# Where the transposes run: attention output by DMA, q and k by TensorE

## The chip, the cores and the metric

The kernel runs on one core of one Trainium2 chip. The metric is the device time of one execution in microseconds (us), and lower is better. Times of several runs of the same program are given with their median; the profile is of one of these executions and goes with that execution's own time.

## The reference

Inputs are q, k and v of shape (8 batches, 8 heads, 576 tokens, 64), and two weights, `moe_w_in` (512 x 2048) and `moe_w_out` (2048 x 512), all float32. Attention is causal within a window of 64 tokens; its output feeds a two-layer network:

```python
scores = (1/8) * q @ k.T                      # per batch and head
mask   = (rel >= 0) & (rel < 64)              # rel = query position - key position
attn   = softmax(where(mask, scores, -1e9))
x      = (attn @ v) -> (4608 tokens, 512)     # heads side by side
h      = x @ moe_w_in
g      = h * sigmoid(1.702 * h)
out    = g @ moe_w_out                        # float32
```

## The kernel before, in words

All matmul operands are bf16. The 4608 tokens are cut into 36 tiles m of 128 tokens, each of two query blocks of 64 tokens (nine blocks to a batch), and into nine chunks of four tiles, 512 tokens.

**Attention of one tile.** `scores(m)` (L243) makes 16 small matmuls, one per head and block: q of 64 tokens against k of 128 tokens, into the PSUM tile S. `exp(m)` (L253, ACT) writes E, `mask(m)` (L258, DVE) multiplies it with a 0/1 band into PT. `pv(m)` (L272) multiplies PT with v; a column of ones beside v gives the row sums. `norm(m)` takes the reciprocal of the sums (L283) and writes the tile xs, 128 tokens x 512, in bf16 (L285, DVE). `x_mm(m)` (L299) transposes xs by four TensorE transposes with the identity `ident` into the PSUM tile pxt, and `x_out(m)` (L307, DVE) copies that into xT, the chunk's transposed x (four blocks of 128 features x 512 tokens). Tacc of `pv` and pxt share one PSUM buffer (pool psT, one buffer).

**The network.** For a chunk ch and one of 16 hidden blocks f, `up_mm` (L318) makes four matmuls, 512 wide, from xT into hps (two buffers); `up_act` makes tanh (L329, ACT) and then gT (L331, DVE). `down_mm` (L338) makes matmuls from gT and w_out into ops (two buffers), 16 for each 128 tokens; `down_out` copies ops to o_sb (L348, ACT) and stores it from the SP queue (L349).

**Transposed q and k.** `scores` needs q and k with the head's 64 features on the partitions: qkt, two buffers, batch b in number b % 2. Two ways lead there.

- The first, for batches 0 and 1: `load_qk` (L74, on POOL's queue, with a cast to bf16) puts nine consecutive tokens in a row of a partition of `raw`. `spread` (L103, four copies on DVE) lays raw into `wide`, in which the other head's half is zero, and five units `qk_mm` (L205) transpose it on TensorE, with wide as weights against the 0/1 matrix `sel`: 16 matmuls in units 0 to 3, eight in unit 4. `qk_out` empties PSUM into qkt: for units 0 to 3 one copy on ACT (L220) and one on DVE (L222); for unit 4 one on ACT (L226), which writes every ninth token. From batch 1 on units use the PSUM tile S, of which there is one and which `scores` uses too. There is one `wide` for q and one for k, and `raw` has two buffers.
- The second, for batches 2 to 7: `load_rows` (L85, ten loads on POOL's queue, with a cast) puts tokens on the partitions, and `turn_rows` (L94, ten DMA transposes on the SP queue) writes qkt.

v comes by `load_v_f32` on the SP queue with `cast_v` on DVE and POOL for batches 0 and 1, and by `load_v` (L126, POOL's queue, with a cast) and `shift_v` (L133 and L134, DVE) later.

**Order.** Each engine runs its own instructions in the order in which the program states them; that order is written by hand. First come loads, the units of batch 0, and attention of tiles 0 to 3. Then a loop over 144 slots (chunk ch, block f): in each slot stand the works filed under `post` (ACT, DVE and DMA work), an output copy where f is a multiple of four, `up_mm` and `up_act` of (ch, f), the TensorE works filed under `pe`, and four `down_mm` of the chunk before. `at(slot, f, after)` files f under `pe` of its slot and `after` under `post` of the next; `later` files under `post`. `period` files scores of the next tile, pv of tile m, the mask, and x_mm two slots on. Tile m of 8 and more has slot 4(m - 4), so there is one attention tile to four slots; tiles 4 to 7 have slots 7, 9, 11 and 13. In the program's order `spread(1)` stands at slot 0, the units of batch 1 in slots 0 to 4. `load_v_f32(1)` is stated before the attention of tile 0.

Of the kernel before, what the change touches and what calls it, by code (L numbers as in the profile page):

```python
# [8 lines left out]
B = 8  # L9
H = 8  # L10
S = 576
D = 64
NTOK = B * S
DM = H * D
DFF = 2048
P = 128
NQB = 9
NM = NTOK // P
NCH = NTOK // 512
RR = 9  # L20
NT = S // RR
PAD = 64

fp32 = mybir.dt.float32
bf16 = mybir.dt.bfloat16
AF = mybir.ActivationFunctionType
ALU = mybir.AluOpType
# [3 lines left out]
def kernel(  # L31
# [9 lines left out]
    nc = tc.nc  # L41
    scale = 1.0 / 8.0

    keep = ctx.enter_context(tc.tile_pool(name="keep", bufs=1))
    ep_pool = ctx.enter_context(tc.tile_pool(name="ep", bufs=2))
    xs_pool = ctx.enter_context(tc.tile_pool(name="xs", bufs=2))
    rc_pool = ctx.enter_context(tc.tile_pool(name="rc", bufs=2))
    xt_pool = ctx.enter_context(tc.tile_pool(name="xt", bufs=3))
    th_pool = ctx.enter_context(tc.tile_pool(name="th", bufs=2))
# [3 lines left out]
    psT = ctx.enter_context(tc.tile_pool(name="psT", bufs=1, space=bass.MemoryType.PSUM))  # L53
# [10 lines left out]
    qkt = [keep.tile([P, 8, PAD + S], bf16, name=f"qkt{i}") for i in range(2)]  # L64
# [7 lines left out]
    def load_qk(b, hps):  # L72
        for w, src in enumerate((q, k)):
            nc.gpsimd.dma_start(  # L74
                out=raw[b % 2][w][:, hps, :],
                in_=src[b].rearrange("(g two) (p r) d -> (two p) g (r d)", two=2, r=RR)[:, hps, :],
            )

    rows = [[keep.tile([P, 5, DM], bf16, name=f"rows_{w}{i}") for w in "qk"] for i in range(2)]

    def load_rows(b):
        for w, src in enumerate((q, k)):
            for i in range(5):
                n = P if i < 4 else 64
                nc.gpsimd.dma_start(  # L85
                    out=rows[b % 2][w][0:n, i, :].rearrange("p (h d) -> p h d", d=D),
                    in_=src[b, :, P * i : P * i + n, :].rearrange("h p d -> p h d"),
                )

    def turn_rows(b):  # L90
        for i in range(5):
            for w in range(2):
                n = P if i < 4 else 64
                nc.sync.dma_start_transpose(  # L94
                    out=qkt[b % 2][:, w::2, PAD + P * i : PAD + P * i + n],
                    in_=rows[b % 2][w][0:n, i, :],
                )

    def spread(b, hps):
        for w in range(2):  # L100
            for par in range(2):
                rows = slice(par * 64, par * 64 + 64)
                nc.vector.tensor_copy(  # L103
                    out=wide[w][rows, hps, :, par, :],
                    in_=raw[b % 2][w][rows, hps, :].rearrange("p g (r d) -> p g r d", d=D),
                )
# [15 lines left out]
    def load_v(b):  # L122
        vn = v_nat[b % 2]
        for i in range(5):
            n = P if i < 4 else 64
            nc.gpsimd.dma_start(  # L126
                out=vn[0:n, i, :, 0:D],
                in_=v[b, :, P * i : P * i + n, :].rearrange("h p d -> p h d"),
            )
# [28 lines left out]
    for base in (0, -64):  # L158
        nc.gpsimd.affine_select(
            out=sel[:], in_=sel[:], compare_op=ALU.not_equal, fill=1.0,  # L160
            base=base, pattern=[[-1, 64]], channel_multiplier=1,
# [4 lines left out]
        out=band[:], in_=band[:], compare_op=ALU.is_ge, fill=0.0,  # L166
        base=64, pattern=[[1, 64]], channel_multiplier=-1,
    )
    nc.gpsimd.affine_select(
        out=band[:], in_=band[:], compare_op=ALU.is_ge, fill=0.0,  # L170
        base=-1, pattern=[[-1, 64]], channel_multiplier=1,
    )
    ident = keep.tile([P, P], bf16, name="ident")
    nc.gpsimd.memset(ident[:], 0.0)
    nc.gpsimd.affine_select(
        out=ident[:], in_=ident[:], compare_op=ALU.not_equal, fill=1.0,
        base=0, pattern=[[-1, P]], channel_multiplier=1,
    )
    for j in range(4):
        load_w_in(j)  # L180
# [47 lines left out]
    def blocks_of(m):  # L228
        return [(t, *divmod(2 * m + t, NQB)) for t in range(2)]

    def s_tile():
        return psS.tile([P, 2, 512], fp32, name="S", tag="S")

    S_of, PT_of, T_of, xs_of, E_of = {}, {}, {}, {}, {}
# [16 lines left out]
    def exp(m):  # L251
        E_of[m] = ep_pool.tile([P, 2, 512], bf16, name="E", tag="E")
        nc.scalar.activation(out=E_of[m][:], in_=S_of.pop(m)[:], func=AF.Exp, scale=scale)  # L253
# [11 lines left out]
    def pv(m):  # L265
        acc = T_of[m] = psT.tile([P, 2, 512], fp32, name="Tacc", tag="T")
        pt = PT_of.pop(m)[:].rearrange("p a f -> p (a f)")
        for h in range(H):
            for t, b, j in blocks_of(m):
                epos = (h % 2) * 512 + t * 256 + (h // 2) * 64  # L270
                win = (v_off if j % 2 == 0 else v_nat)[b % 2][:, j // 2, h, 0 : D + 1]
                nc.tensor.matmul(  # L272
                    acc[t * 64 : t * 64 + 64, h // 4, (h % 4) * 66 : (h % 4) * 66 + 65],
                    lhsT=pt[:, epos : epos + 64],
                    rhs=win,
                    start=True,
                    stop=True,
                )

    def norm(m):  # L280
        view = T_of.pop(m)[:, :, 0:264].rearrange("p b (h e) -> p b h e", e=66)
        rc = rc_pool.tile([P, 2, 4, 1], fp32, name="rc", tag="rc")
        nc.vector.reciprocal(out=rc[:], in_=view[:, :, :, D : D + 1])  # L283
        xs = xs_of[m] = xs_pool.tile([P, DM], bf16, name="xs", tag="xs")
        nc.vector.tensor_tensor(  # L285
            out=xs[:].rearrange("p (b h d) -> p b h d", b=2, h=4),
            in0=view[:, :, :, 0:D],
            in1=rc[:].to_broadcast([P, 2, 4, D]),
            op=ALU.mult,
        )  # L290

    xT = {}
    X_of = {}

    def x_mm(m):
        ps = X_of[m] = psT.tile([P, 4, P], bf16, name="pxt", tag="T")
        xs = xs_of.pop(m)
        for c in range(4):
            nc.tensor.transpose(  # L299
                out=ps[:, c, :], in_=xs[:, c * P : (c + 1) * P], identity=ident[:, :]  # L300
            )

    def x_out(m):
        ch = m // 4
        if m % 4 == 0:
            xT[ch] = xt_pool.tile([P, 4, 512], bf16, name="xT", tag="xT")
        nc.vector.tensor_copy(  # L307
            out=xT[ch][:, :, (m % 4) * P : (m % 4) * P + P], in_=X_of.pop(m)[:]
        )


# [40 lines left out]
    def pair(pool, shape_tag):  # L352
        return [pool.tile([P, 512], fp32, name="qk", tag=shape_tag)[:] for _ in range(2)]

    for u in range(5):
        if u % 2 == 0 and u < 4:
            spread(0, slice(u, u + 2))
        if u == 0:
            s = s_tile()
            p = [s[:, 0, :], s[:, 1, :]]  # L360
        elif u == 1:
            s = psT.tile([P, 2, 512], fp32, name="Tq", tag="T")
            p = [s[:, 0, :], s[:, 1, :]]
        elif u == 2:
            p = pair(psH, "H")
        elif u == 3:
            p = pair(psO, "O")
        else:
            p = [psH.tile([P, 512], fp32, name="qk", tag="H")[:]]
# [7 lines left out]
    for m in range(4):  # L377
        scores(m)
        exp(m)
        mask(m)  # L380
        if m > 0:
            x_mm(m - 1)
            x_out(m - 1)
        pv(m)
        norm(m)
    x_mm(3)
    x_out(3)

# [3 lines left out]
    def at(slot, f, after=()):  # L394
        pe.setdefault(slot, []).append(f)
        for g in after:
            post.setdefault(slot + 1, []).append(g)

    def later(slot, g):
        post.setdefault(slot, []).append(g)  # L400

    def qk_unit(slot, b, u):
        box = {}

        def mm():
            s = s_tile()
            box["p"] = [s[:, 0, :], s[:, 1, :]]
            qk_mm(b, u, box["p"])

        at(slot, mm, [lambda: qk_out(b, u, box["p"])])  # L410

    def period(slot, m, nxt):
        if nxt is not None:
            at(slot, lambda: scores(nxt), [lambda: exp(nxt)])
        at(slot, lambda: pv(m), [lambda: norm(m)])
        if nxt is not None:
            later(slot + 2, lambda: mask(nxt))
        at(slot + 2, lambda: x_mm(m), [lambda: x_out(m)])

    later(0, lambda: spread(1, slice(0, 4)))  # L420
    for u in range(5):
# [3 lines left out]
    def slot_of(m):  # L425
        return (7, 9, 11, 13)[m - 4] if m < 8 else 4 * (m - 4)

    for m in range(4, NM):
        period(slot_of(m), m, m + 1 if m + 1 < NM else None)

    for b in range(2, B):
        last_pv = slot_of((9 * (b - 1) - 1) // 2)
        later(last_pv + 1, lambda b=b: load_v(b))
        later(slot_of(9 * b // 2), lambda b=b: shift_v(b))
        turn_at = slot_of((9 * (b - 1) - 1) // 2 - 1) + 2
        later(turn_at, lambda b=b: turn_rows(b))
        later(5 if b < 4 else slot_of((9 * (b - 3) - 1) // 2 - 1) + 3, lambda b=b: load_rows(b))

    for ch in range(NCH):
        for f in range(16):  # L440
            s = 16 * ch + f
# [49 lines left out]
```

## Time and profile before

| | |
|---|---|
| time, three runs | 357.15 us median (355.5 to 358.89) |
| the profiled execution's own time | 358.89 us |
| its span, first to last instruction | 357.2 us |
| mean granted TensorE clock | 0.989 |
| PE busy | 304.4 us (85%), 2592 matmuls |
| DVE busy | 207.3 us (58%) |
| ACT busy | 151.7 us (42%) |
| POOL busy | 94.7 us (27%) |
| DMA moved | 36.47 MB in 134910 packets, 124128 of them under 512 B |

How to read it: PE is TensorE's matmuls and PEld its weight loads, DVE VectorE, ACT ScalarE, POOL GpSimd, and SP the queue that issues the stores and transposes. A row of a list in order of time gives start, duration, engine, source line, operation, output <- input, the count, and in brackets how long the engine was idle before and what ended that. A row of a group gives shapes and count, then the busy time in us and the mean of one in ns, then the idle time before. Matmuls are pipelined, so the distance between starts tells more of the time that they hold PE than the durations do.

### The profile page before, as it was taken

Reading aid. Unit: us, or ns where it says so; the run is one execution under the profiler, and the core shown is the slowest. Engines: PE = TensorE matmul, PEld = TensorE weight load, DVE = VectorE, ACT = ScalarE, POOL = GpSimd, SP = SyncE. Lnnn points to the kernel's source line nnn. Section 1 sums busy time; section 2 is a strip of 40 time slices with the busy share of each in tenths; the row PEclk is TensorE's granted clock in tenths of the full one; section 3 lists DMA queues with packets and bytes.
Section 4 is the critical chain, followed back from the end, with each engine's and each line's share of the span. In section 5 each row is a group of like instructions: output and inputs, shape, how many; then the busy total and the mean of one; then the engine's idle time right before and its main releaser. Section 6 shows DMA issues by size and latency. Waiting matters only on the chain.

```text
span 357.2 us, 6403 instructions
## 1 busy us (share of the span) xinstructions
PE 304.4 (85%) x2592; PEld 152.4 (43%) x2592; DVE 207.3 (58%) x339; ACT 151.7 (42%) x227; POOL 94.7 (27%) x118
## 2 busy tenths in 40 slices
PE   0034467767999999999999999999999999999995
PEld 0023333433444444444444444445444544444442
DVE  7876577675665675556655755566657565533400
ACT  1015213953445444555444444555454444444411
POOL 8061069954690026314921000010000000000000
PEclk9999998998999999999999999999999999999999
DMA  8999959999999299979994843771000000010021
GB/s 145 196 187 196 201 93 128 151 143 138 155 175 118 71 111 149 122 119 134 146 115 66 119 88 46 119 111 55 35 31 32 30 31 29 31 59 29 31 88 60
DMA packets 134910, 36.47 MB, mean 102 GB/s; under 512 B 124128, under 2 KB 130272, under 8 KB 134880
## 3 DMA queue, kind: packets, MB, share of 16 engines
q0 software_dynamic: 90752, 17.18, 61.1%
q1 hardware_dynamic: 44128, 18.88, 24.0%
q8 instruction: 20, 0.33, 0.4%
q14 instruction: 10, 0.08, 0.1%
HBM read 36.70 MB, written 9.44 MB: 129 GB/s over the span
## 4 chain that ended last, share of the span: by engine, by line
PE 74%; DVE 12%; issue 5%; ACT 4%; DMA 2%; POOL 2%; DVEq 0%; POOLq 0%; ACTq 0%
PE ops L338 33%; PE hps L318 30%; PE Tacc L272 4%; PE S L243 3%; DMA rows_k<-in_k_dram 2%; PE pxt L299 2%; DVE wide_k L103 2%; DVE v_off L133 2%; ACT qkt L226 1%; DVE v_off L192 1%; DVE v_nat L191 1%; POOL rows_q L85 1%; ACT E L253 1%; ACT th L329 1%; DVE PT L258 1%
## 5 line engine op out<-in xcount | busy, mean ns | idle before, releaser
L331 DVE SCALAR_TENSOR_TENSOR gT<-th,hps 128x512 bf16<-128x512 bf16 x144 | 99.0, 688 | 113.0 <-ACT th L329 112.6
L318 PE MATMUL hps<-xT,w_in_sb 128*128 128x512 bf16 x576 | 151.2, 387 | 2.4 <-DVE xT L307 2.4
L329 ACT ACTIVATE th<-hps 128x512 bf16<-128x512 f32 x144 | 86.3, 599 | 143.7 <-PE hps L318 137.9
L338 PE MATMUL ops<-w_out_sb,gT 128*128 128x512 bf16 x576 | 146.4, 381 | 0.0
L318 PEld LDWEIGHTS <-w_in_sb 128*128 128x128 bf16 x576 | 56.5, 99 | 69.9 <-issue 6.0
L338 PEld LDWEIGHTS <-gT 128*128 128x128 bf16 x576 | 53.0, 98 | 56.4 <-issue 0.8
L253 ACT ACTIVATE E<-S 128x1024 bf16<-128x1024 f32 x36 | 36.7, 1019 | 7.5 <-PE S L243 7.4
L85 POOL DMA_DIRECT2D rows_q<-in_q_dram x30 | 26.5, 892 | 50.2 <-DMA qkt<-rows_q 39.3
L126 POOL DMA_DIRECT2D v_nat<-in_v_dram x30 | 25.3, 869 | 52.1 <-PE Tacc L272 49.7
L348 ACT ACTIVATE o_sb<-ops 128x512 f32<-128x512 f32 x36 | 21.5, 597 | 20.0 <-PE ops L338 20.0
L85 POOL DMA_DIRECT2D rows_k<-in_k_dram x30 | 27.0, 924 | 4.2 <-DMA v_nat<-in_v_dram 2.5
L285 DVE TENSOR_TENSOR xs<-Tacc,rc 128x512 bf16<-128x512 f32 x36 | 24.9, 691 | 1.2
L205 PE MATMUL S<-sel,wide_q 128*128 128x64 bf16 x44 | 3.7, 242 | 22.7 <-DVE wide_q L103 20.2
L272 PE MATMUL Tacc<-v_off,PT 128*64 128x65 bf16 x320 | 17.4, 203 | 6.2 <-DVE xT L307 3.2
L258 DVE TENSOR_TENSOR PT<-E,mask_None 128x1024 bf16<-128x1024 bf16 x28 | 19.2, 685 | 2.0 <-ACT E L253 2.0
L272 PEld LDWEIGHTS <-PT 128*64 128x64 bf16 x576 | 13.7, 116 | 13.9 <-DVE PT L258 6.5
L243 PE MATMUL S<-qkt 64*128 64x64 bf16 x576 | 15.5, 196 | 4.2 <-ACT qkt L226 4.2
L272 PE MATMUL Tacc<-v_nat,PT 128*64 128x65 bf16 x256 | 15.1, 205 | 4.5 <-DVE xT L307 4.5
L243 PEld LDWEIGHTS <-qkt 64*128 64x128 bf16 x576 | 11.1, 98 | 17.1 <-issue 13.9
L205 PEld LDWEIGHTS <-wide_q 128*128 128x128 bf16 x72 | 5.2, 131 | 27.7 <-DVE wide_q L103 23.2
L299 PE MATMUL pxt<-ident,xs 128*128 128x128 bf16 x144 | 14.8, 229 | 2.5 <-DVE xs L285 2.5
L299 PEld LDWEIGHTS <-xs 128*128 128x128 bf16 x144 | 11.2, 102 | 10.7 <-DVE xs L285 3.3
(50 smaller groups left out, 113.4 us busy)
## 6 DMA issues: line engine op xcount, KB each, us to landing
out_dram<-o_sb SPq DMA_DIRECT2D x36, 256.0 KB, 2.1
rows_q<-in_q_dram POOLq DMA_DIRECT2D x24, 128.0 KB, 5.7
rows_k<-in_k_dram POOLq DMA_DIRECT2D x24, 128.0 KB, 6.2
v_nat<-in_v_dram POOLq DMA_DIRECT2D x24, 128.0 KB, 5.3
v_f<-in_v_dram SPq DMA_DIRECT2D x8, 256.0 KB, 12.5
w_in_sb<-in_moe_w_in_dram POOLq DMA_DIRECT2D x4, 512.0 KB, 14.0
w_out_sb<-in_moe_w_out_dram POOLq DMA_DIRECT2D x4, 512.0 KB, 14.8
raw_q<-in_q_dram POOLq DMA_DIRECT2D x2, 288.0 KB, 7.2
```

Source lines behind the costliest of these rows:

```text
L85: nc.gpsimd.dma_start(out=rows[b % 2][w][0:n, i, :].rearrange("p (h d) -> p h d", d=D), in_=src[b, :, P * i : P * i + n, :].rearrange("h p ...
L126: nc.gpsimd.dma_start(out=vn[0:n, i, :, 0:D], in_=v[b, :, P * i : P * i + n, :].rearrange("h p d -> p h d"),)
L243: nc.tensor.matmul(st[:, h % 2, t * 256 + hp * 64 : t * 256 + hp * 64 + 64], lhsT=src[rows, 2 * hp + 1, 64 * j : 64 * j + 128], rhs=src[ro ...
L253: nc.scalar.activation(out=E_of[m][:], in_=S_of.pop(m)[:], func=AF.Exp, scale=scale)
L258: nc.vector.tensor_tensor(out=pt[:].rearrange("p a f -> p (a f)"), in0=E_of.pop(m)[:].rearrange("p a f -> p (a f)"), in1=masks[z][:].rearr ...
L272: nc.tensor.matmul(acc[t * 64 : t * 64 + 64, h // 4, (h % 4) * 66 : (h % 4) * 66 + 65], lhsT=pt[:, epos : epos + 64], rhs=win, start=True, ...
L285: nc.vector.tensor_tensor(out=xs[:].rearrange("p (b h d) -> p b h d", b=2, h=4), in0=view[:, :, :, 0:D], in1=rc[:].to_broadcast([P, 2, 4, D]),
L299: nc.tensor.transpose(out=ps[:, c, :], in_=xs[:, c * P : (c + 1) * P], identity=ident[:, :])
L318: nc.tensor.matmul(ps[:, :], lhsT=w_in_sb[:, c, f * P : (f + 1) * P], rhs=xT[ch][:, c, :], start=(c == 0), stop=(c == 3),)
L329: nc.scalar.activation(out=th[:], in_=ps[:], func=AF.Tanh, scale=0.851)
L331: nc.vector.scalar_tensor_tensor(out=g[:], in0=th[:], scalar=1.0, in1=ps[:], op0=ALU.add, op1=ALU.mult)
L338: nc.tensor.matmul(O_of[ch, tsub][:, :], lhsT=gT[ch, f][:, tsub * P : (tsub + 1) * P], rhs=w_out_sb[:, f, :], start=(f == 0), stop=(f == 15),)
```

## The change

Batches 2 to 7 get q and k by the first way, as batches 0 and 1: `load_rows` and `turn_rows` go; `spread`, the five units and `qk_out` of each batch are filed in slots after `plan`. The units of batch 2 stand in slots 6, 8, 10, 12 and 14. For batches 3 to 7 units 0 to 3 stand two slots after an attention tile (slots 2, 6, 10 ... of four), unit 4 in the slot after unit 3, and that is the last slot before the first scores that need the batch. `spread(b)` is filed in the slot of unit 0, after the mask.

The attention output takes the DMA: `x_mm` and `x_out` go, with `ident`, and `x_turn(m)` issues one DMA transpose of xs into xT on the SP queue right after `norm(m)`. xs has four buffers in place of two.

```diff
-    xs_pool = ctx.enter_context(tc.tile_pool(name="xs", bufs=2))
+    xs_pool = ctx.enter_context(tc.tile_pool(name="xs", bufs=4))
...
-    def load_rows(b):
...
-    def turn_rows(b):
...
-    ident = keep.tile([P, P], bf16, name="ident")
...
-    def x_mm(m):
-        ps = X_of[m] = psT.tile([P, 4, P], bf16, name="pxt", tag="T")
-        xs = xs_of.pop(m)
-        for c in range(4):
-            nc.tensor.transpose(
-                out=ps[:, c, :], in_=xs[:, c * P : (c + 1) * P], identity=ident[:, :]
-            )
-
-    def x_out(m):
+    def x_turn(m):
         ch = m // 4
         if m % 4 == 0:
             xT[ch] = xt_pool.tile([P, 4, 512], bf16, name="xT", tag="xT")
-        nc.vector.tensor_copy(
-            out=xT[ch][:, :, (m % 4) * P : (m % 4) * P + P], in_=X_of.pop(m)[:]
+        nc.sync.dma_start_transpose(
+            out=xT[ch][:, :, (m % 4) * P : (m % 4) * P + P], in_=xs_of.pop(m)[:]
         )
...
         mask(m)
-        if m > 0:
-            x_mm(m - 1)
-            x_out(m - 1)
         pv(m)
         norm(m)
-    x_mm(3)
-    x_out(3)
+        x_turn(m)
...
-        at(slot, lambda: pv(m), [lambda: norm(m)])
+        at(slot, lambda: pv(m), [lambda: norm(m), lambda: x_turn(m)])
...
-        at(slot + 2, lambda: x_mm(m), [lambda: x_out(m)])
...
-    for b in range(2, B):
-        last_pv = slot_of((9 * (b - 1) - 1) // 2)
-        later(last_pv + 1, lambda b=b: load_v(b))
-        later(slot_of(9 * b // 2), lambda b=b: shift_v(b))
-        turn_at = slot_of((9 * (b - 1) - 1) // 2 - 1) + 2
-        later(turn_at, lambda b=b: turn_rows(b))
-        later(5 if b < 4 else slot_of((9 * (b - 3) - 1) // 2 - 1) + 3, lambda b=b: load_rows(b))
+    free = [s for s in range(14, 16 * NCH) if s % 4 == 2]
+    spare = [s for s in range(14, 16 * NCH) if s % 4 == 3]
+    first = {b: 4 * ((9 * b) // 2 - 5) for b in range(2, B)}
+    plan = {2: [(6, 0), (8, 1), (10, 2), (12, 3), (14, 4)]}
+    for b in range(3, B):
+        last = first[b]
+        slots = [s for s in free if s < last][-4:]
+        plan[b] = [(s, u) for u, s in enumerate(slots)]
+        plan[b].append(([s for s in spare if s < last][-1], 4))
+    for b, todo in plan.items():
+        later(todo[0][0], lambda b=b: spread(b, slice(0, 4)))
+        for s, u in todo:
+            qk_unit(s, b, u)
+        later(slot_of((9 * (b - 1) - 1) // 2) + 1, lambda b=b: load_v(b))
+        later(slot_of(9 * b // 2), lambda b=b: shift_v(b))
+    later(5, lambda: load_qk(2, slice(0, 4)))
+    for b in range(3, B):
+        later(plan[b - 2][-1][0] + 2 if b > 3 else 6, lambda b=b: load_qk(b, slice(0, 4)))
```

More of the change, by code (lines that the diff above doesn't have):

```diff
@@ L77, in load_qk @@
             )
-    rows = [[keep.tile([P, 5, DM], bf16, name=f"rows_{w}{i}") for w in "qk"] for i in range(2)]
-    def load_rows(b):
[L82 to L87, printed above, removed]
-                )
-    def turn_rows(b):
[L91 to L97, printed above, removed]
     def spread(b, hps):
@@ L171 @@
         base=-1, pattern=[[-1, 64]], channel_multiplier=1,
-    )
-    ident = keep.tile([P, P], bf16, name="ident")
[L174 to L177, printed above, removed]
     )
@@ L292 @@
     xT = {}
-    X_of = {}
-    def x_mm(m):
-        ps = X_of[m] = psT.tile([P, 4, P], bf16, name="pxt", tag="T")
-        xs = xs_of.pop(m)
-        for c in range(4):
-            nc.tensor.transpose(
-                out=ps[:, c, :], in_=xs[:, c * P : (c + 1) * P], identity=ident[:, :]
-            )
-    def x_out(m):
+    def x_turn(m):
         ch = m // 4
```

## The prediction

> **What bounds the kernel now.** I read the page's busy shares, then busy time by stage, then the order of time on PE, DVE and SP, then the groups for the pieces that the change multiplies. The stages (PE, PEld, DVE, ACT and POOL busy, clock, DMA share, GB/s; the DMA share can pass 1):
>
> ```profile
> 45.00:99.00 54.00, 39.91 (x412) 21.14 (x413) 36.85 (x58) 24.32 (x34) 37.80 (x41) 0.94 1.77 134
> 99.00:306.00 207.00, 206.37 (x1750) 100.86 (x1749) 124.22 (x217) 100.48 (x155) 42.69 (x51) 1.00 0.74 89
> ```
>
> From 99 us on PE is busy 206.4 of 207: each microsecond put on its queue, or each wait, lengthens the run. Before that PE idles 14 of 54 us. PE and DVE in order of time, one steady period:
>
> ```profile
> 131.96 1.03 PE L318 MATMUL hps<-xT,w_in_sb 128*128 128x512 bf16 x4
> 132.82 0.39 PE L299 MATMUL pxt<-ident,xs 128*128 128x128 bf16 x4
> 133.05 1.03 PE L338 MATMUL ops<-w_out_sb,gT 128*128 128x512 bf16 x4
> ...
> 132.53 0.68 DVE L258 TENSOR_TENSOR PT<-E,mask_None 128x1024 bf16<-128x1024 bf16 x1
> 133.65 0.69 DVE L331 SCALAR_TENSOR_TENSOR gT<-th,hps 128x512 bf16<-128x512 bf16 x1 [0.44 <-ACT th L329]
> ```
>
> The start-to-start times count, since matmuls overlap: four x transposes hold PE 133.05 - 132.82 = 0.23 us, four 512-wide matmuls 0.86. A slot is 4 up plus 4 down, 1.73 us. Between the mask and gT (0.44 us of idle DVE) the new copies will stand. The front, by SP, DVE and PE in order of time:
>
> ```profile
> 31.58 14.70 SPq L111 DMA_DIRECT2D v_f<-in_v_dram  x5
> 46.18 1.51 DVE L103 COPY wide_q<-raw_q 64x2304 bf16<-64x2304 bf16 x2
> 47.72 3.12 DVE L103 COPY wide_k<-raw_k 64x2304 bf16<-64x2304 bf16 x2
> ...
> 50.90 0.61 PE L205 MATMUL S<-sel,wide_k 128*128 128x64 bf16 x8 [2.29 <-DVE wide_k L103]
> ```
>
> SP issues batch 1's v until 46.28; and one spread of batch 1 (4.6 us on DVE) makes PE wait. That is the pattern the change repeats for six batches.
>
> **The Trainium skill.** "TensorE: Matmul & The Clock Gate", Part 2, step 1: matmuls stay in program order, only weight loads are pulled ahead. The trace agrees (the row at 50.90 stops the up matmuls behind it), so a PE wait for DVE can't be filled. Same page, "HAM oscillation": an idle stretch of about a window of 3.4 us halves the clock. Agrees in part: after 1.85 us without work at 83.6 to 85.46, and gaps before it, four down matmuls took 89.01 - 87.33 = 1.68 us, not 0.86; that spell lost 1.4 us. "VectorE: DVE Perf Modes", "The three transpose paths": TensorE is the shorter transpose, the DMA one 1309 ns. SP here holds 1.21 us for each 128x512 one, and landing takes longer still.
>
> **The change, part by part.** Sum made on the profiled execution: 358.89 us, span 357.2 and 1.7 around it.
>
> *Front* (up to the first up matmuls of chunk 1, now at 85.46). (a) Attention of m = 0 to 3: pv of m waits for the xT copy of m-1, a chain of 3.37 us per m (40.15 to 43.51). Without the copy 0.36 goes, three times, and the last xs ends at 44.1; but (b) shows that nothing can use it before 46.28: 0. (b) The four x transposes stand on SP behind batch 1's v, so none issues before 46.28. At the 1.3 us between transposes in the trace the fourth issues at 50.2. Landing took 2.3 us at the least, 2.5 to 3.4 (medians) late in the run, 7.7 beside the loads of 48 to 92 us; the new raw loads start at 50.2 too, so I take 4 (ends 2.3 and 7.7). Up of chunk 0 starts at 54.2, not 46.31: +7.9. (c) Slots 0 to 5 took 19.55 us. Spread of batch 1 now hides under that wait, and slot 0 falls from 5.0 to 2.56, and the rest keeps its order and its durations (batch 1's v casts, 3 us on DVE, and unit 4's 2.4 us copy among them): 16.8, so -2.7. (d) Slots 6 to 15 took 19.6. Spread of batch 2 stands between mask and gT at slot 6, and PE is stopped until 5.15 us into it, where two slots had taken 2.5. From there the one S tile passes from scores (exp 1.03) to a unit (ACT copy 0.59, then DVE 0.69, behind gT and mask): 4.2 us per pair of slots, as the 4.36 now. x of m = 7: norm ends 20.9 us after slot 6 starts, its DMA lands 3.5 later, so up of chunk 1 comes at 24.2: +4.6. The pxt and xT waits (7.8 us of pv waiting) go, but the S tile takes their place. Front: 7.9 - 2.7 + 4.6 = **+9.8**, ends +5 and +14 (mostly the landing, 2.3 to 7.7). If the wait in b were gone, spread 1 would lie open again: b and c go together.
>
> *Steady.* (e) 27 x 0.22 us of x transposes leave PE: -5.9. The xT copies (418 ns) leave DVE, which is not the bound: 0. (f) Batches 3 to 7 get 72 transposing matmuls each. At half clock 8 took 0.43 us (53.01 to 53.45), 54 ns each, which is the 64 columns; at full clock 27, I take 28: 5 x 72 x 28 ns = +10.1. Ends 27 and 54 (half clock kept, or the 128-column weight load binding): +9.7 and +19.4. (g) Spread. In the period shown it is queued after mask, so it starts 133.1; four copies of 0.76 us (1.51 for two) end at 136.2. The first unit stands on PE at 132.82 and its last eight matmuls wait for wide_k: it ends 136.45 instead of 133.27. Behind it stand the down matmuls and all later slots: 3.2 us per batch, +16. gT of that slot is late too, but its hps buffer is wanted two slots on: 0. In batches 3 and 5 POOL's next raw load is released by these copies, and its issue lies beside wide_k; beside POOL's cast one copy took 2.37 us, beside issues a half-size one 0.74 instead of 0.45: 0.5 twice, +1.0. Ends of g: 14 and 22. (h) Unit 4's ACT copy takes 2.4 us (row below) and holds both S and qkt, which the next slot's scores need. In the period shown tanh of unit 4's slot ends at 135.5, the copy at 137.9, and scores are due after up at 136.7: 1.2 us, five times, +6 (ends 4 and 8). The output copy and tanh queued behind it on ACT end at 139.1, gT at 139.8, before the up matmuls that want their buffer: 0 more. (i) Clock: a stop of 3.2 us is longer than the 1.85 that halved it; 1.4 us lost per spell, in three of five: +4 (ends 0 and 8). (j) x of the last m of a chunk: xs ends 3.4 us after its slot starts, the DMA lands 2.5 to 3.4 later, up wants it 7.7 after: hidden, 0; cover is 1 to 2 us, a landing of 5 would cost 0.7 at each of 7 chunks. On SP each transpose (1.21 us) stands one slot after an output store whose o_sb copy ends 0.6 us into the slot: no hold-up; a transpose waits for its xs with only the next store behind it. The new wait of xs for the transpose four tiles back is long over. On POOL raw loads of batch b+2 wait for spread of b, with v loads behind them that no one needs for 16 slots or more: 0. (k) SP loses 60 transposes, POOL the 60 row loads, 128 KB each in 256-byte pieces, and gets 12 of 576 KB: PE didn't wait for them after 99 us, so 0. (l) The copies of units 0 to 3, four of 0.69 us on DVE and four of 0.59 on ACT per batch, fall in the last slot of a period, where DVE has only gT and idles about 1 us of 1.73, ACT 0.9: they hide there, and S is free again before the next scores: 0; without that cover 0.7 us each.
>
> ```profile
> L226 ACT CAST qkt<-S 128x512 bf16<-128x512 f32 x1 | 2.4, 2403 | 0.0
> L103 DVE COPY wide_q<-raw_q 64x2304 bf16<-64x2304 bf16 x2 | 1.5, 750 | 0.0
> L103 DVE COPY wide_k<-raw_k 64x2304 bf16<-64x2304 bf16 x2 | 3.1, 1554 | 0.0
> ```
>
> Steady: -5.9 + 10.1 + 17 + 6 + 4 = **+31.2**. Together +41.0: 399.9 against 358.9. The median shown, 357.15, is 1.7 lower, so the forecast is 398.
>
> **Rivals.** *A, smaller stops:* transposes land in 2.3 us, so the front costs +5; DVE reaches the copies 1.2 us earlier (g = 10), h = 4, no clock loss: 5 - 5.9 + 10.1 + 10 + 4 = +23, about 380. For it: DVE is busy 124 of 207 us. Against: DVE works in order and the copies stand behind a mask. *B, everything dear:* beyond the forecast, front +4.2, f at 40 ns +4.3, the clock in all five spells +3, x late at each chunk +5, spread 1 dearer each time +5: +21.5, about 419. For it: landings of 7.7 and the 2.37 us copy; against: DMA share 0.74 in the steady part. *C, faster:* the front's 14 us of idle PE is made by the DMA share of 1.77 (row loads released late, shift of batch 2 waiting for v), and the change frees it. Price: -14, with -5.9 and +10.1, no other stop: 347. It decides if spread, unit 4 and the SP queue together stop PE less than 10 us. Against it: the waits in 65 to 85 us name DVE xT, not a DMA, and unit 0 already waited for spread. That x isn't turned by DMA is no case: all 36 transposes stand in the code.
>
> **How the numbers follow.** Forecast 0.62, A 0.16, B 0.18, C 0.04. Leaving out C and the outer half of A's and B's tails gives 377 to 415. Within 1% of 357 (about what a measurement can tell from no change) only a mixture with C's relief falls: 0.02; faster 0.03; slower 0.95.
>
> **What would show it.** Right: the first unit's matmuls waiting some 3 us for wide_k in six batches; scores waiting about 1.2 us for the 2.4 us copy; up of chunk 0 starting near 54 us, released by the transpose DMA; 72 matmuls per batch in 2.0 us; half-clock spells after the stops. Wrong: PE 99% busy from 105 us on, or up of each chunk waiting for xT. A front that ends before 90 us (up of chunk 1) speaks for A; matmuls of 50 ns for B.

## The result, and the profile after

The changed kernel takes 404.59 us (median of four runs, 401.52 to 405.18), beside 357.36 for the kernel before on the same chip: 1.1307 times as long, 95% interval 1.1228 to 1.1386. The forecast was 398, the range 377 to 415. The profiled execution took 404.34 us with a span of 402.5 and a mean granted clock of 0.975; the one before took 358.89 with 357.2 and 0.989. So 45.3 us of span have to be found between the two traces, where the prediction's sum said 41.0.

The border between its two parts, the first up matmuls of chunk 1, moved from 85.46 to 102.35 us. The front costs 16.9 us (forecast 9.8), the rest 28.4 (forecast 31.2): 300.15 us from there to the end, where 271.7 were.

Busy time by stage, after; the columns are those of the same view before (PE, PEld, DVE, ACT and POOL busy, clock, DMA share, GB/s):

```profile
45.00:116.00 71.00, 39.24 (x429) 20.37 (x430) 37.73 (x58) 26.70 (x37) 16.30 (x19) 0.88 0.79 103
116.00:351.00 235.00, 217.63 (x2033) 107.60 (x2032) 141.83 (x230) 122.67 (x183) 19.83 (x24) 0.99 0.41 68
```

PE was busy 206.4 of 207 us in the long stage; now it is 217.6 of 235. It works more and it also stops. Against the long stage before, the DMA share has fallen from 0.74 to 0.41 and POOL's busy time has halved; no gain in time shows from either.

The front in order of time, SP and PE, after:

```profile
31.93 15.46 SPq L91 DMA_DIRECT2D v_f<-in_v_dram  x5
47.43 5.23 SPq L272 DMA_TRANSPOSE xT<-xs  x4
...
58.87 1.87 PE L283 MATMUL hps<-xT,w_in_sb 128*128 128x512 bf16 x4 [15.37 <-DMA xT<-xs]
...
102.35 1.31 PE L283 MATMUL hps<-xT,w_in_sb 128*128 128x512 bf16 x4 [2.74 <-issue]
```

The four x transposes stand behind batch 1's v on SP, as step b said. The last is issued at 51.45, and PE, idle for 15.4 us, starts when it has landed, 7.3 us later. The three others took 2.4 to 2.8. Row 102.35 is the border, up of chunk 1. The landing of the four x tiles over this stretch, after:

```profile
DMA to landing us min/median/max: 2.4/2.6/7.3
```

One steady period in order of time (batch 6), PE above and DVE below, after:

```profile
238.25 1.03 PE L283 MATMUL hps<-xT,w_in_sb 128*128 128x512 bf16 x4
240.99 0.41 PE L179 MATMUL S<-sel,wide_q 128*128 128x64 bf16 x8 [1.72 <-DVE wide_q L83]
242.55 0.41 PE L179 MATMUL S<-sel,wide_k 128*128 128x64 bf16 x8 [1.15 <-DVE wide_k L83]
242.79 1.81 PE L303 MATMUL ops<-w_out_sb,gT 128*128 128x512 bf16 x4
...
238.82 0.68 DVE L232 TENSOR_TENSOR PT<-E,mask_None 128x1024 bf16<-128x1024 bf16 x1
239.42 1.52 DVE L83 COPY wide_q<-raw_q 64x2304 bf16<-64x2304 bf16 x2
240.97 1.52 DVE L83 COPY wide_k<-raw_k 64x2304 bf16<-64x2304 bf16 x2
```

This is the picture the forecast drew for step g: mask, four copies, and PE standing at each pair of them. Without the wait the unit would stand at 239.1 (238.25 and four matmuls) and end 0.46 later, at 239.6; it ends at 242.79, so 3.2 us are lost. The four matmuls from 242.79 on take 1.6 us and the next four, from 244.39, 1.7, not 0.86: the granted clock is 0.50 for a spell.

The waits of PE from 102.4 us on, after (total us, times, longest):

```profile
PE S L179 <- DVE wide_q L83: 8.6, 5, 1.7
PE S L179 <- DVE wide_k L83: 5.9, 5, 1.2
PE S L217 <- ACT qkt L200: 5.2, 5, 1.0
```

Five batches, three waits each, 19.7 us in all. The third line is step h. The copy that it waits for, after:

```profile
L200 ACT CAST qkt<-S 128x512 bf16<-128x512 f32 x7 | 16.9, 2411 | 0.0
```

### The profile page after: what moved, and what is told of

It reads as the page before. It is cut to its first block, busy times and chain, and to the rows that moved or that the text cites. A ratio compares the mean times of both kernels' runs of the same rounds, so it can differ in the third digit from the quotient of the medians.

```text
span 402.5 us, 6925 instructions
## 1 busy us (share of the span) xinstructions
PE 313.8 (78%) x2880; PEld 157.1 (39%) x2880; DVE 226.1 (56%) x351; ACT 176.4 (44%) x257; POOL 49.8 (12%) x68
## 4 chain that ended last, share of the span: by engine, by line
PE 66%; DVE 18%; ACT 9%; issue 4%; DMA 2%; SPq 1%; DVEq 0%; ACTq 0%
PE ops L303 29%; PE hps L283 27%; ACT qkt L200 4%; PE Tacc L246 4%; DVE wide_k L83 3%; PE S L179 3%; PE S L217 3%; DVE wide_q L83 3%; ACT th L294 3%; DVE PT L232 2%; DMA xT<-xs 2%; DVE gT L296 2%; ACT E L227 1%; DVE v_off L166 1%; DVE v_nat L165 1%
## 5 line engine op out<-in xcount | busy, mean ns | idle before, releaser
L283 PE MATMUL hps<-xT,w_in_sb 128*128 128x512 bf16 x576 | 153.7, 391 | 18.1 <-DMA xT<-xs 15.4
L303 PE MATMUL ops<-w_out_sb,gT 128*128 128x512 bf16 x576 | 148.1, 385 | 0.0
L283 PEld LDWEIGHTS <-w_in_sb 128*128 128x128 bf16 x576 | 56.3, 100 | 86.0 <-issue 24.2
L179 PE MATMUL S<-sel,wide_q 128*128 128x64 bf16 x260 | 15.2, 200 | 34.5 <-DVE wide_q L83 31.1
L194 ACT CAST qkt<-S 128x512 bf16<-128x512 f32 x29 | 17.0, 585 | 43.6 <-PE S L179 43.4
L179 PEld LDWEIGHTS <-wide_q 128*128 128x128 bf16 x288 | 15.2, 105 | 47.7 <-DVE wide_q L83 37.0
L313 ACT ACTIVATE o_sb<-ops 128x512 f32<-128x512 f32 x36 | 23.2, 643 | 19.1 <-PE ops L303 19.1
L217 PE MATMUL S<-qkt 64*128 64x64 bf16 x576 | 15.9, 199 | 12.9 <-ACT qkt L200 9.3
L196 DVE CAST qkt<-S 128x512 bf16<-128x512 f32 x29 | 20.0, 689 | 5.4 <-ACT qkt L194 5.4
L217 PEld LDWEIGHTS <-qkt 64*128 64x128 bf16 x576 | 12.0, 99 | 27.5 <-issue 21.6
L179 PE MATMUL S<-sel,wide_k 128*128 128x64 bf16 x260 | 15.3, 201 | 7.5 <-DVE wide_k L83 7.5
L179 PEld LDWEIGHTS <-wide_k 128*128 128x128 bf16 x288 | 13.5, 106 | 10.4 <-DVE wide_k L83 9.4
L200 ACT CAST qkt<-S 128x512 bf16<-128x512 f32 x7 | 16.9, 2411 | 0.0
## 6 DMA issues: line engine op xcount, KB each, us to landing
v_f<-in_v_dram SPq DMA_DIRECT2D x8, 256.0 KB, 12.6
```

The source lines that it names most:

```text
L179: nc.tensor.matmul(dst[:, col * 64 : col * 64 + 64], lhsT=wide[w][:, hp, r, :, :].rearrange("p two d -> p (two d)"), rhs=sel[:], start=Tru ...
L200: nc.scalar.copy(out=o, in_=i)
L217: nc.tensor.matmul(st[:, h % 2, t * 256 + hp * 64 : t * 256 + hp * 64 + 64], lhsT=src[rows, 2 * hp + 1, 64 * j : 64 * j + 128], rhs=src[ro ...
L283: nc.tensor.matmul(ps[:, :], lhsT=w_in_sb[:, c, f * P : (f + 1) * P], rhs=xT[ch][:, c, :], start=(c == 0), stop=(c == 3),)
L303: nc.tensor.matmul(O_of[ch, tsub][:, :], lhsT=gT[ch, f][:, tsub * P : (tsub + 1) * P], rhs=w_out_sb[:, f, :], start=(f == 0), stop=(f == 15),)
```

## The experiments

The first six kernels are the changed one with one edit each; two put edits together; the last two start from the kernel before. Ratios are to the kernel before, with 95% intervals. That kernel, run again beside each, had medians of 357.4 to 357.7, so the times can also be set beside the changed kernel's 404.59. Each trace is of a single execution.

### The wide copies earlier

```diff
-        later(todo[0][0], lambda b=b: spread(b, slice(0, 4)))
+        if b == 2:
+            later(todo[0][0], lambda b=b: spread(b, slice(0, 4)))
+        else:
+            for i in range(4):
+                before = 1 if i > 1 else 3 - b % 2
+                later(todo[0][0] - before, lambda b=b, i=i: spread_one(b, i))
```

> The changed kernel, but for batches 3 to 7 the four spread copies are filed one to three slots before the first unit, two and two, instead of in its slot; batch 2 is left. Forecast's theory (the stop before the first unit is the price, 3.2 us five times, and it brings two half-clock spells of 1.7 us): 404.6 - 16 - 3.4 + 1 to 2 for delayed gT = 386 to 388 us, PE's waits for wide in the steady part under 2 us, full clock there. Rival (DVE has no room, the copies only push gT and the masks, and PE waits for those instead): gain under 8 us, 397 or more, with PE waiting for gT or PT.

Measured: 385.52 us, ratio 1.0768 (1.0687 to 1.0848), 19.1 below the changed kernel. A unit of the same phase, PE in order of time, with the copies earlier:

```profile
223.97 0.40 PE L187 MATMUL S<-sel,wide_q 128*128 128x64 bf16 x8
224.20 0.40 PE L187 MATMUL S<-sel,wide_k 128*128 128x64 bf16 x8
224.43 1.03 PE L311 MATMUL ops<-w_out_sb,gT 128*128 128x512 bf16 x4
```

The 16 matmuls take 0.46 us, 29 ns each, and nothing waits. In the steady part the waits for wide, 14.5 us in the changed kernel, are all gone, and so is the half clock after them. All the copies are still done, and so are all the matmuls: what cost the time was the place of the copies, not their work. How much of the 19.1 us belongs to it is less sharp. The profiled execution, at 381.15 us the fastest of the four, is 23.2 below the changed kernel's; 6.2 of these lie in the front, which this edit leaves alone (up of chunk 1 at 96.16, not 102.35; "The turns before the loads" shows why), and 17.0 behind it. That is about the 16.1 of stops and 3.4 of half clock, less 1.5 for an x tile late at one chunk and 1.2 more of pv waiting for `v_off`.

### Batch 1's v by POOL's queue

```diff
-    load_v_f32(1)
...
+    load_v(1)
...
-    later(2, lambda: cast_v(1))
+    later(2, lambda: shift_v(1))
```

> The changed kernel, but v of batch 1 is loaded with a cast on POOL's queue and shifted, as v of batches 2 to 7, so that SP is free for the x transposes of tiles 0 to 3. Theory 1 (the transposes stand behind batch 1's v on SP, and that makes the first 12.6 us): they issue right after each norm, 35 to 44.5 us, land 2.5 to 3 us later, up of chunk 0 starts at 47 to 48 instead of 58.9, and the run takes 393 to 395 us. Theory 2 (the landing of 7.3 us beside the loads is the larger half, SP's queue only the smaller): the issue moves to 44.5, the landing stays 6 to 8 us since the weights' loads still run, up of chunk 0 at 51 to 53, 397 to 399 us. A rival for which neither counts, the front being held by DVE: 402 or more.

Measured: 400.12 us, ratio 1.1209 (1.1148 to 1.1271), 4.5 below. SP and PE in order of time, with v by POOL:

```profile
37.24 10.30 SPq L272 DMA_TRANSPOSE xT<-xs  x4
...
56.32 0.59 PE L283 MATMUL hps<-xT,w_in_sb 128*128 128x512 bf16 x1 [10.98 <-DMA xT<-xs]
```

SP is free, and the first transpose is issued ten microseconds earlier. The up projection still comes only 2.5 us earlier, because now all four land late (the trace has 7.9 to 11.1 us from issue to landing, 9.9 for the last): POOL's loads are under way all the while. Both theories expected more, in time and for chunk 0; theory 2 came nearer. At chunk 0, freeing SP's queue gains little, since the landing grows by most of what the queue gave back. The 2.5 us there, and the 4.2 by which up of chunk 1 comes earlier (98.13), are within the scatter of the front between executions, shown under "The turns before the loads".

### q and k alone

The q and k half of the change, with x transposed on TensorE as before (xs with two buffers, `ident`, `x_mm` and `x_out` put back).

> One half of the change alone: q and k of batches 2 to 7 by raw loads, spread and units as in the changed kernel, but x by four matmuls and a PSUM copy as before. Theory (nearly all of the loss is in the q and k half): the front gets back the 12.6 us before chunk 0 but shows spread of batch 1 again (+2.4) and pv waits for the xT copies beside the S tile (+2 to 4), so up of chunk 1 comes at 95 to 97; the steady part gets 27 x 0.22 = 5.9 us more on PE: 402 to 406 us, the same as the changed kernel. Rival (x's DMA is the main loss): 375 us or less.

Measured: 403.99 us, ratio 1.1306 (1.1233 to 1.1379): the change without its x half is as slow as the change. In its trace the span is 399.8 and up of chunk 1 starts at 93.28:

```profile
93.28 1.08 PE L299 MATMUL hps<-xT,w_in_sb 128*128 128x512 bf16 x4 [3.16 <-DVE xT L288]
```

So in the profiled executions the x half costs 9.1 us in the front (102.35 against 93.28) and saves 6.4 after it (306.5 against 300.15), where step e had 5.9. The 9.1 is of a slow front: other traces with the changed front have up of chunk 1 at 96.2 to 101.4. The medians, 0.6 apart, say that the two sides about cancel.

### The fifth unit's copy on two engines

```diff
-            nc.scalar.copy(out=o, in_=i)
+            if b < 3:
+                nc.scalar.copy(out=o, in_=i)
+            else:
+                nc.scalar.copy(out=o[:, 0:4], in_=i[:, 0:4])
+                nc.vector.tensor_copy(out=o[:, 4:8], in_=i[:, 4:8])
```

> The changed kernel, but unit 4's copy into qkt is halved for batches 3 to 7: four of the eight blocks on ACT, four on DVE. Theory (scores wait about 1.04 us five times for the 2.4 us ACT copy): ACT takes 1.2 us, DVE's half lies beside it if a strided 2-byte write costs it about the same, the waits go, 404.6 - 4 to 5 = 400 to 401 us. Rival (DVE's half comes later than ACT's whole did, since it stands behind gT, or its strided write is slow): scores wait for DVE instead, 404 or more.

Measured: 404.69 us, ratio 1.1319 (1.1230 to 1.1407); nothing gained, a miss. ACT, DVE and PE in order of time, with the copy split:

```profile
138.53 1.29 ACT L203 CAST qkt<-S 128x256 bf16<-128x256 f32 x1
139.85 1.28 DVE L204 CAST qkt<-S 128x256 bf16<-128x256 f32 x1 [0.51 <-ACT qkt L203]
141.19 0.41 PE L221 MATMUL S<-qkt 64*128 64x64 bf16 x16 [1.23 <-DVE qkt L204]
```

Each half takes half the time, but DVE, idle before, starts 0.03 us after ACT has ended: the sum is what it was. The Trainium skill's "PSUM — Partial Sum Buffer", in its section on PSUM bank collisions, says that two engines may not touch one bank on the same partitions at once, and that software puts a wait between them, for two readers too. The trace has such a wait, but does not show the bank to be its reason. DVE's copies of two other units in order of time, in the changed kernel:

```profile
28.40 0.69 DVE L196 CAST qkt<-qk 128x512 bf16<-128x512 f32 x1 [0.16 <-PE qk L179]
...
62.25 0.69 DVE L196 CAST qkt<-S 128x512 bf16<-128x512 f32 x1 [0.15 <-ACT qkt L194]
```

In the second (unit 0 of batch 1) ACT and DVE read different halves of S, 512 columns each, and DVE still starts 0.03 us after ACT has ended. In the first (unit 3 of batch 0) each half is a PSUM tile of its own, and DVE starts while ACT's copy runs on to 28.56, though both write the same qkt. So in these traces the wait goes with the shared PSUM tile. The fifth unit with two tiles was not run.

Why a copy of 512 columns takes 2.41 us here, and 0.585 in the other units, is not a matter of the engine: both halves are as slow on theirs. It writes every ninth token, 18 bytes apart, and the Trainium skill's "Advanced Engine Details and Errata", SBUF Cachelines, has a penalty where each access falls in another line of 16 bytes. The two durations would fit that; no run here changes the step.

### The fifth unit first

```diff
-        plan[b] = [(s, u) for u, s in enumerate(slots)]
-        plan[b].append(([s for s in spare if s < last][-1], 4))
+        slots.append([s for s in spare if s < last][-1])
+        plan[b] = list(zip(slots, (4, 0, 1, 2, 3)))
```

> The changed kernel, with the fifth unit of turns of batches 3 to 7 (the one whose ScalarE copy takes 2.4 us) done first of the five, two slots ahead, and the four others in the slots after it. The spread copies are filed with the first unit, as before. Theory 1, the 1.0 us stop of TensorE behind that copy is one of order only, since in the new place the next scores' tile is free in time or the copy lies beside more TensorE work: the five stops, 5.2 in the trace, go, and the time is 399-400. Theory 2, whichever unit has the copy, the scores of the next tile wait for it: 404-405, with the stop at another place.

Measured: 400.07 us, ratio 1.1177 (1.1126 to 1.1228), 4.5 below, near the 5.2 of the trace. In its trace the waits of scores for the 2.4 us copy are gone from the steady part, and the waits for wide stand (8.6 and 6.9 us, where they were 8.6 and 5.9). Step h was a matter of order. The profiled execution, at 401.82 us the slowest of the four, shows less of the gain: four of its five stops for wide are followed by half clock, not two, and the part after the border is only 1.6 shorter.

### The turns before the loads

POOL reads one column of each of the four x tiles, and so waits for them, before it issues batch 2's loads.

```diff
+    def hold():
+        for t in range(4):
+            nc.gpsimd.tensor_copy(out=held[:, t : t + 1], in_=xT[0][:, 0, P * t : P * t + 1])
+
+    held = keep.tile([P, 4], bf16, name="held")
+    later(5, hold)
     later(5, lambda: load_qk(2, slice(0, 4)))
```

> The changed kernel, with POOL made to wait for the four x tiles of chunk 0 before it issues batch 2's loads of q and k. In the changed kernel the fourth of those tiles landed 7.3 us after its issue, in the moment in which these loads begin, where 2.4 to 2.6 us are usual. Theory 1, the tile waits behind the loads' traffic: it lands in about 2.5, the up projection of chunk 0 starts near 54 in place of 58.9, and the time falls by 2 to 5, to 400-402. Theory 2, the landing has nothing to do with these loads: the up projection starts at 58 to 59 and the time stays at 404, or rises, since the loads come later and slot 6 waits longer for them.

Measured: 400.82 us, ratio 1.1181 (1.1107 to 1.1255), 3.8 below. PE busy, clock, DMA share and GB/s while the last tile is on its way, first in the changed kernel:

```profile
53.00:55.00 2.00, 0.00 (x0) 1.00 0.91 138
55.00:57.00 2.00, 0.00 (x0) 1.00 1.20 196
```

and with the turns before the loads:

```profile
53.00:55.00 2.00, 1.54 (x5) 1.00 0.03 8
```

In the first, POOL's raw loads begin at 51.14, just before the transpose, and the DMA engines fill up. In the second they are held until 53.64. Its landings, and the matmul that waited:

```profile
DMA to landing us min/median/max: 2.4/2.6/2.9
...
53.23 0.58 PE L283 MATMUL hps<-xT,w_in_sb 128*128 128x512 bf16 x1 [10.06 <-DMA xT<-xs]
```

All four land in under 3 us, and up of chunk 0 starts at 53.23 instead of 58.87; 0.8 of these 5.6 us come from SP, which was free earlier in this execution, and 4.8 from the landing. Only the loads' time of issue differs by the edit (and four tiny copies on POOL), so the loads are the cause of the late landing.

Other traces bear this out and show the scatter. The last of the four tiles took 2.4 to 2.5 us in all three traces with the hold (this one and the two below). Without it, in the four traces whose front is that of the changed kernel, the landing goes with the order of two issues: where POOL's first raw load was issued 0.2 to 0.3 us ahead of the last transpose, it took 7.3 (changed kernel) and 7.1 (fifth unit first); where the load was issued 0.2 to 0.3 us behind it, 4.2 (wide copies earlier) and 4.8 (copy on two engines). Up of chunk 0 started at 58.87, 57.92, 53.66 and 56.20. So a part of the front's cost is luck of the execution. The Trainium skill's "DMA: Bandwidth & Descriptors", Issuing engines are not separate DMA queues, says that DMAs of all issuing engines run on the same 16 DMA engines and interleave: a transpose on SP's queue is no way around POOL's loads.

### The amendments together

The early wide copies, the fifth unit first, the hold, and batch 2's wide copies one slot earlier.

```diff
+        if b == 2:
+            later(todo[0][0] - 1, lambda b=b: spread(b, slice(0, 4)))
...
+        plan[b] = list(zip(slots, (4, 0, 1, 2, 3)))
...
+    later(5, hold)
```

> The changed kernel with three amendments together: the wide copies of batches 3 to 7 filed one to three slots ahead of the first unit, two and two (batch 2's one slot ahead), the fifth unit first, and the loads of batch 2 held until the four x tiles of chunk 0 have landed. If the stops are separate terms they add up: 404.6 - 19 (wide copies) - 5 (fifth unit) - 3 (landing) - 3 (slot 6), 374 to 378. If one hides behind another: 380 to 386. If the change had no cost besides these, it would come to 357; what remains over that is the five units a batch themselves and the front.

Measured: 379.65 us, ratio 1.0597 (1.0546 to 1.0649), above the range in which the gains just add, and just below the other one. The weight load ahead of the first up matmul of chunk 1 in order of time, and the landing of that chunk's last two x tiles, in this kernel:

```profile
97.70 0.14 PEld L291 LDWEIGHTS <-w_in_sb 128*128 128x128 bf16 x2 [9.08 <-issue]
...
DMA to landing us min/median/max: 8.3/9.0/9.6
```

PE stops for 8.6 us there, where the changed kernel stops 2.7: chunk 1's last tile, issued at 88.1, met loads that POOL had issued from 79.4 to 90.6. So the amendments moved the loads from one turn on to another. A second hold, for chunk 1's tiles, ahead of the loads of q and k of batch 4 and of v of batch 3:

```diff
+    later(15, lambda: hold(1))
```

> The kernel with the three amendments together took 379.7, 2 to 6 above the sum of the single gains: its trace shows TensorE stopped for 8.6 us ahead of the up projection of chunk 1, with the last x tile of that chunk issued at 88.1 and landed 9.6 later, while POOL's loads (q and k of batch 4, v of batch 3) were under way. Here POOL waits, ahead of those loads, for the four x tiles of chunk 1, as it does for those of chunk 0 ahead of batch 2's. Theory 1, an x tile lands late because loads are under way: it lands in 2.5 to 3, 6 of the 8.6 go, and some of the half clock after the stop; 370 to 374. Theory 2, the late landing has another cause, or the loads only meet another tile: 378 to 381.

Measured: 374.37 us, ratio 1.0491 (1.0419 to 1.0563), 5.3 less, 0.4 above what theory 1 gave. The weight load again, and the landing of the last two x tiles, with the second hold:

```profile
93.36 0.14 PEld L291 LDWEIGHTS <-w_in_sb 128*128 128x128 bf16 x2 [5.01 <-DMA xT<-xs]
...
DMA to landing us min/median/max: 5.5/7.4/9.3
```

The last tile lands in 5.5 us instead of 9.6, where 2.5 to 3 were expected, and PE's stop is shorter by as much, 4.1 us, not by 6. Loads issued before 77 us were still under way when it was issued at 87.8 (the last of them landed at 92.9), and POOL waits only ahead of later ones.

Of what is left over 357, half lies in the front: in its trace up of chunk 1 starts at 93.39, 7.9 later than before, which isn't broken down here. The rest takes 279.4, 7.7 more, and that is accounted for to within a microsecond: 10.5 for the units' matmuls, less the x matmuls, 6.4 as measured above, and waits of pv for `v_off`, 3.7 where before had 1.0; together 6.8.

### x alone, in the kernel before

q and k as before, by rows and DMA transposes; x by DMA from tile 8 on, and the turns of q and k of batches 4 to 7 filed one to a slot.

```diff
-        at(slot, lambda: pv(m), [lambda: norm(m)])
+        at(slot, lambda: pv(m), [lambda: norm(m)] + ([lambda: x_turn(m)] if m > 7 else []))
...
-        at(slot + 2, lambda: x_mm(m), [lambda: x_out(m)])
+        if m < 8:
+            at(slot + 2, lambda: x_mm(m), [lambda: x_out(m)])
```

> The kernel before, with q and k loaded by rows and turned by DMA transposes as there, and the x half of the change alone, from tile 8 on (chunks 2 to 7): x of those tiles is turned by a DMA transpose on SP, and the turns of q and k of batches 4 to 7 are filed one a slot instead of ten at once, so that an x tile does not queue behind ten of them. Theory 1, the x half gains its TensorE work where the tile lands in time: 24 tiles x 0.22 us, 5.3 us below before, 352. Theory 2, x tiles wait on SP or land late beside the row loads, and TensorE stops at chunk boundaries: 357 to 365.

Measured: 357.69 us, ratio 0.9995 (0.9963 to 1.0028): no difference. (There are 28 such tiles, not 24, so theory 1 should have said 6.2.) PE in order of time at chunk 4's start, and the landing of the x tile issued at 176.5, x by DMA from tile 8 on:

```profile
183.72 1.02 PE L326 MATMUL hps<-xT,w_in_sb 128*128 128x512 bf16 x4 [2.67 <-issue]
...
DMA to landing us min/median/max: 7.1/7.1/7.1
```

The tile landed 7.1 us after its issue, beside row loads and v loads, and PE stood 2.7 us for it; the slots after it lost some 1.2 more, at a lower clock (seven big matmuls took 2.7 us, not 1.5). The profiled span fell by 2.4, about what 6.2 less those two leaves.

```diff
-        at(slot, lambda: pv(m), [lambda: norm(m)] + ([lambda: x_turn(m)] if m > 7 else []))
+        at(slot, lambda: pv(m), [lambda: norm(m)] + ([lambda: x_turn(m)] if m > 19 else []))
...
-        if m < 8:
+        if m < 20:
```

> The kernel before with x turned by DMA from tile 20 on in place of tile 8 on, so only in chunks 5 to 8, where the profile shows the DMA engines with little to do. With tile 8 on, the time did not move: the trace shows 2.7 us of TensorE stopped ahead of chunk 4, for an x tile that landed 7.1 us after its issue beside the row loads, and slow matmuls after it. Theory 1, the x half gains 0.22 us a tile wherever the tile lands in time: 16 tiles, 3.5 us, 353.5 to 355. Theory 2, TensorE's time for the four transposes was not on the path, or the gain is taken back elsewhere: 357 to 358.

Measured: 354.2 us (22 runs), ratio 0.9926 (0.9901 to 0.9950). It is faster than both kernels, by 3.2 us against the kernel before, close to the 3.5 that 16 tiles of 0.22 us make. The turns of q and k filed one to a slot, which this kernel shares with the last, were not run alone; in the kernel before PE waited for no turn in this part. The landings of all its x tiles, and PE's only wait from 104 us on:

```profile
DMA to landing us min/median/max: 2.3/2.3/4.2
...
PE Tacc L272 <- DVE v_off L133: 0.4, 2, 0.2
```

No tile is late and no chunk waits.

## Why the prediction was right, and where its sizes were off

The sign and the place of the losses were right; the sum fell 4.3 us short of the profiled difference. The front was 7.1 too low and the steady part 2.8 too high, so the total came nearer than its parts, which is luck.

**Front, +16.9 measured, +9.8 forecast.** *a* held: the last xs gained nothing, since SP was not free. *b* was the term mis-sized most: +12.6 instead of +7.9. SP came free 1.1 us later than in the trace before, the fourth transpose left 1.25 later than taken (51.45, not 50.2), and its landing took 7.3 instead of the 4 chosen between 2.3 and 7.7. The prediction had written down why it could be near the upper end (the raw loads start at the same time) and chose a middle value all the same. That the loads made it late is shown by holding them (4.8 us of landing in the trace, 3.8 us in the median). That it was 7.3 and not 4 was luck of this execution: with the same front three others had 4.2, 4.8 and 7.1, and reached up of chunk 1 at 96.2, 99.3 and 101.4, so that the front cost 10.7 to 15.9 there. *c* was right: slots 0 to 5 took 16.3, forecast 16.8 (19.55 less the 5.0 - 2.56 that it names would be 17.1). *d* was short: slots 6 to 15 took 27.2, forecast 24.2. The stop at slot 6 took 5.4 (forecast 5.15), x of tile 7 landed 3.7 after its norm (forecast 3.5), but that norm came 2.5 late; 0.3 of this is the stop, and most of the rest a spell of half clock from 80.6 to 86, where two times four up matmuls take 1.8 and 1.7 us. The prediction priced such spells in the steady part and forgot them in the front.

**Steady, +28.4 measured, +31.2 forecast.** *e*: 6.4 saved, forecast 5.9; the x tiles after the border number 28, not 27, at 0.23 us each. *f*: 29 ns a matmul, so 10.5 instead of 10.1. *g*: 3.2 us a batch as worked out, five times 16; but the 1.0 for POOL's issue beside the copies was 0.1, the dearer copies of two batches taking 0.85 instead of 0.755. With *i* it makes 19.5; the early copies gave back 19.1 in the median and, with the waits that they brought set against it, 17.0 in the trace. *h*: 5.2, forecast 6. *i*: 3.4, forecast 4. The Trainium skill's "TensorE: Matmul & The Clock Gate", HAM oscillation, lets an idle stretch of about a window of 3.4 us halve the clock; here two shorter idles (1.7 and 1.15 us) with eight small matmuls between did it after two of the five stops, batches 3 and 6, for 1.7 us each. What tells them from the others is when they fall. In these traces the granted clock changes only at steps of 3.41 us. Busy time of the engines, clock, DMA share and GB/s for the steps around the stops of batch 4 and batch 6, after (columns as above):

```profile
154.15:157.56 3.41, 2.09 (x10) 0.77 (x8) 2.73 (x5) 1.19 (x2) 0.00 (x0) 1.00 0.17 38
157.56:160.97 3.41, 1.86 (x22) 1.12 (x23) 2.93 (x5) 0.59 (x1) 0.00 (x0) 1.00 0.00 0
...
239.48:242.89 3.41, 0.75 (x17) 0.64 (x18) 3.32 (x6) 0.43 (x1) 0.00 (x0) 1.00 0.00 0
242.89:246.30 3.41, 3.41 (x12) 1.22 (x8) 1.01 (x2) 0.59 (x1) 0.00 (x0) 0.50 0.02 5
```

Batch 4's stop is split over two steps, and PE is busy for over half of each; batch 6's lies in one, with PE busy for 0.75 of 3.41 us, and the next step has half clock. Over the twelve traces of this case a full-clock step with PE busy for less than 0.41 of it was always followed by half clock, one with more than 0.46 never; between the two both occur. So the number of spells is chance: in the six traces that have these five stops it is two, two, three, three, four and four. The forecast's three of five stood in the middle.

*j* held: after chunk 1 no chunk waits for xT, with landings of 2.3 to 8.1 us. *k* and *l* held. The measured terms add to 28.8: 16.1 + 10.5 + 5.2 + 3.4 - 6.4.

**Rivals.** A needed g near 10 and a landing of 2.3, and had neither. B's landings of 7 us came, in the front and twice after it (8.1 and 6.9 us), but after up of chunk 1 no chunk waited for one; f stayed at 29 ns. C's point of decision was that the stops together stay below 10 us; they came to 21. The DMA share of the front did fall, from 1.77 to 0.79, but the front grew by 16.9 us: the turns of x stand on its path and meet what loads remain. Whether DMA traffic made any of the idle time of the front before was not tested by itself.

## What to carry to other kernels

A copy in the order of an engine that isn't the bound costs its full length where the bounding engine's next instruction reads it: 17 us in the trace, 19 in the median, went by filing the same four copies one to three slots earlier. A DMA on the critical path should be priced at its landing beside whatever else the DMA engines carry in that moment (here 2.3 to 2.9 us with little else, 4 to 11 beside loads), not at its median; moving work off the bounding engine on to DMA paid here only where they had little else to carry (3.2 us from tile 20 on, nothing from tile 8 on). When several repairs are put together, look again at what each of them sets free to start.

## What the runs showed of the hardware that was not expected

- The landing of a 128x512 bf16 DMA transpose from SBUF to SBUF ran from 2.3 to 11.1 us, by what else was on the DMA engines; SP's own time for issuing it was 1.19 us in most cases (up to 1.84 in the changed kernel). The last x tile of chunk 0 took over 7 us in the two traces where a load was issued 0.2 to 0.3 us ahead of it, and under 5 in the two where the load came 0.2 to 0.3 us behind; issued up to ten microseconds earlier, but beside loads, the tiles of chunk 0 let PE start only 2.5 us earlier.
- Two copies out of one S tile by ACT and DVE ran one after the other (DVE's began 0.03 us after ACT's end), so a split copy took 2.6 us instead of 2.4. Out of two PSUM tiles they overlapped by 0.16 us.
- Of five equal stops of PE, 1.7 and 1.15 us with eight matmuls between, two were followed by half clock: those that lay within one 3.41 us step of the granted clock, with PE busy for 1.08 and 0.75 us of it. The three that were split over two steps, with PE busy for 1.68 us or more in each, were not.
